# A decode block's feed-forward weights: w2 thirteen rows to a partition, w1 in two transfers, h1 in two passes

## The chip, the core and the metric

The kernel runs on one core of a Trainium2 chip. The metric is the device time of one execution in microseconds, the median of several runs. A core has TensorE (PE; the loads of its stationary operand are shown as PEld), VectorE (DVE), ScalarE (ACT), GpSimd (POOL) and SyncE (SP), and 16 DMA engines that move data between HBM and SBUF.

## The reference

One decode step of a transformer block for 4 sequences: attention over a cache of 4096 positions with 32 heads of 128, then a feed-forward layer with the Mish activation, both with a layer norm ahead and a residual.

```python
x = A_x                                             # 4 x 1 x 640, bf16
h = x + _A_ref(_layernorm(x), k_cache, v_cache, wq, wo)
h2 = h + _B_ref(_layernorm(h), w1, b1, w2)          # w1 640 x 1728, w2 1728 x 640

def _B_ref(x, w1, b1, w2):
    h = x @ w1 + b1
    sp = log1p(exp(-abs(h))) + where(h > 0, h, 0)
    return (h * tanh(sp)) @ w2
```

The caches hold 2 x 4 x 32 x 4096 x 128 bf16 values, 268 MB of the 283 MB that the kernel reads.

## The kernel before

The attention runs over 16 units (`u`, eight heads of one sequence). For each, K (8.4 MB, `kt`) and V (`vt`) are loaded into one of three large SBUF slots by SP's queue (`load_kv`, L89). VectorE multiplies K by q (L263), TensorE adds up over the head dimension (L270), VectorE reduces (L251), softmax follows, and TensorE multiplies by V (`pv`, L325). The order is written out by hand (`manual_schedule`), and each engine runs its instructions in the order of the program.

The end of the kernel is where the change lies. When the last K has been used, its slot becomes `wend`, which takes the four blocks of wo (L388) and then w1 (L389); when the V before the last has been used, its slot becomes `wend2`, which takes w2 (L396, L397, L399) and all the small buffers of the end (`scratch`). The last V comes in four quarters. All of these are issued by SP in this order, and the DMA engines serve SP's queue in order.

w1 has 640 rows, which stand as five blocks of 128 partitions (`dc`), each row 1728 columns. The 1728 columns of h1 are cut into chunks of 128, thirteen of them and a fourteenth of 64 (`FREM`). `f_chunk(rows, c)` gives the columns of chunk c; before, these are adjacent columns. The result h1 has the columns of a chunk on its partitions, the chunk and the sequence in the free dimension: `h1_ps[f, c, n]`. For each chunk the five blocks are added up (L491), with w1 as the stationary operand, a load of 128 x 128 for each matmul of 4 columns. After the fifth chunk comes the variance of the layer norm (L469, with Sqrt at L501 and a switch of ACT's table to Exp at L504). VectorE and ScalarE then scale, add b1 and apply Mish (L511 to L537), and y2T (L547) multiplies by w2, whose row for partition p of chunk c must be the same f. b1 is brought into the same order by 14 small matmuls near the start (L213), also by `f_chunk`. The residual (L555), a transpose (L559) and a copy (L567) lead to the output DMA (L568).

w2 is loaded before as one row to a partition and chunk: chunk 12 (`w2s_sb`), then the 64 odd rows (`w2r_sb`), then three groups of four chunks.

Of the kernel before, what the change touches and what calls it, by code (L numbers as in the profile page):

```python
# [16 lines left out]
def kernel(  # L17
# [13 lines left out]
    nc = tc.nc  # L31

    B, Sq, D = A_x.shape
    _, H, Sk, Dh = A_k_cache.shape
    F = B_w1.shape[1]
    N = B * Sq
    DC = D // 128
# [16 lines left out]
    CT = 128 // (G * RQ)  # L54
    VQ = 4

    CI = 4
    CK = F // (128 * CI)
    FM = CK * CI * 128
    C2 = F // 128  # L60
    FREM = F - C2 * 128
    FC = C2 + 1

    ctx.enter_context(tc.manual_schedule())

# [13 lines left out]
    def slot(name):  # L79
        return slots.tile([128, SLOT], BF16, tag="kv", name=name)  # L80
# [36 lines left out]
    nc.vector.memset(nscale[:, :], -SCALE)  # L117
    b1T = consts.tile([128, FC], FP32)
    nc.gpsimd.memset(b1T[:, :], 0.0)
# [38 lines left out]
    for src, dst in ((ln1_v, xT), (x_v, xT_res)):  # L158
# [10 lines left out]
        out=own1[:, :], in_=ident[:, :].rearrange("p (i k) -> p i k", i=G), axis=AX.X, op=ALU.add  # L169
    )  # L170
    nc.vector.tensor_scalar(
        out=own[:, :], in0=own1[:, :], scalar1=-1.0, scalar2=1e30, op0=ALU.add, op1=ALU.mult
    )
    nc.vector.tensor_reduce(
        out=sel[:, :, :],
        in_=ident[:, :].rearrange("p (t i r) -> p r i t", t=CT, r=RQ),
# [5 lines left out]
        out=dq_f[:, :], in_=ident[:, :].rearrange("p (q j) -> p q j", j=J), axis=AX.X, op=ALU.add  # L182
# [4 lines left out]
        out=j_f[:, :], in_=ident[:, :].rearrange("p (q j) -> p j q", j=J), axis=AX.X, op=ALU.add  # L187
# [1 line left out]
    nc.vector.tensor_copy(out=j_m[:, :], in_=j_f[:, :])  # L189

    def f_chunk(rows, c):
        if c < CK * CI:
            k, i = divmod(c, CI)
            block = rows[:, k * 128 * CI : (k + 1) * 128 * CI]
            return block.rearrange("p (i f) -> p i f", i=CI)[:, i, :], 128
        return rows[:, c * 128 : min(F, (c + 1) * 128)], min(F - c * 128, 128)


    qT_ps = ps.tile([128, H, N], FP32, tag="qq", name="qT_ps")
    for h in range(H):  # L200
        for c in range(DC):
# [4 lines left out]
                start=(c == 0),  # L206
                stop=(c == DC - 1),
            )
    nc.scalar.copy(out=qT[:, :, :], in_=qT_ps[:, :, :])
    b_ps = ps.tile([128, FC], FP32, tag="oT", name="b_ps")  # L210
    for c in range(FC):
        cols, fw = f_chunk(b1_row, c)
        nc.tensor.matmul(  # L213
            b_ps[0:fw, c : c + 1], lhsT=cols, rhs=ident[0:1, 0:1], start=True, stop=True
        )
    nc.vector.tensor_copy(out=b1T[:, 0:C2], in_=b_ps[:, 0:C2])  # L216
    nc.vector.tensor_copy(out=b1T[0:FREM, C2:FC], in_=b_ps[0:FREM, C2:FC])

# [165 lines left out]
    w1_sb = wend[:, nwo : nwo + DC * F].rearrange("p (c f) -> p c f", c=DC)  # L384
    e0 = nwo + DC * F
    wo_view = A_wo.rearrange("(o p j) n -> p o j n", o=NO, j=J)
    for o in range(NO):
        nc.sync.dma_start(out=wo_sb[:, o], in_=wo_view[:, o])  # L388
    nc.sync.dma_start(out=w1_sb, in_=B_w1.rearrange("(c p) n -> p c n", p=128))  # L389
    wend2 = slot("wend2")  # L390
    nw2 = FC * D
    w2_sb = wend2[:, 0 : CK * CI * D].rearrange("p (k i n) -> p k i n", k=CK, i=CI)
    w2s_sb = wend2[:, CK * CI * D : C2 * D]
    w2r_sb = wend2[0:FREM, C2 * D : FC * D]
    w2_view = B_w2[0:FM, :].rearrange("(k i p) n -> p k i n", k=CK, i=CI)
    nc.sync.dma_start(out=w2s_sb, in_=B_w2[FM : C2 * 128, :])  # L396
    nc.sync.dma_start(out=w2r_sb, in_=B_w2[C2 * 128 : F, :])  # L397
    for k in range(CK):
        nc.sync.dma_start(out=w2_sb[:, k], in_=w2_view[:, k])  # L399

    at = [nw2]

    def scratch(n, dt=FP32):
        a = at[0]
        w = n * (2 if dt == FP32 else 1)
        w += w % 2
        at[0] = a + w
        ap = wend2[:, a : a + w]
        return ap.bitcast(FP32)[:, 0:n] if dt == FP32 else ap[:, 0:n]
# [53 lines left out]
    def column_means(src, name):  # L463
        part = scratch(N)
        nc.vector.tensor_reduce(
            out=part, in_=src.rearrange("p c n -> p n c"), axis=AX.X, op=ALU.add
        )
        m_ps = ps.tile([128, N], FP32, tag="oT", name=f"{name}_ps")
        nc.tensor.matmul(m_ps[:, :], lhsT=mean_f, rhs=part, start=True, stop=True)  # L469
        return m_ps  # L470
# [4 lines left out]
    for dst in (h2T, hc):  # L475
        nc.vector.tensor_tensor(
            out=dst,
# [7 lines left out]
    h1_ps = ps.tile([128, FC, N], FP32, tag="qq", name="h1_ps")  # L485
    nc.vector.memset(h1_ps[FREM:128, FC - 1, :], 0.0)
    rstd = scratch(N)
    for c in range(FC):
        fw = f_chunk(w1_sb[:, 0, :], c)[1]
        for dc in range(DC):  # L490
            nc.tensor.matmul(  # L491
                h1_ps[0:fw, c, :],
                lhsT=f_chunk(w1_sb[:, dc, :], c)[0],
                rhs=h2T[:, dc, :],
                start=(dc == 0),
                stop=(dc == DC - 1),
            )
        if c == 4:
            v_ps = column_means(sq, "var")
            std = scratch(N)  # L500
            nc.scalar.activation(  # L501
                out=std, in_=v_ps[:, :], func=ACT.Sqrt, bias=eps_t[:, :], scale=1.0
            )
            nc.scalar.activation(out=dummy[:, :], in_=eps_t[0:N, :], func=ACT.Exp)  # L504
            nc.vector.reciprocal(out=rstd, in_=std)

    def fcn():
        return scratch(FC * N).rearrange("p (c n) -> p c n", c=FC)
# [3 lines left out]
        out=h1n,  # L512
# [6 lines left out]
        out=h1s,  # L519
# [8 lines left out]
        out=tb, in0=ta, scalar=2.0, in1=ta, op0=ALU.add, op1=ALU.mult  # L528
# [3 lines left out]
        out=tc_, in0=tb, scalar1=-0.5, scalar2=-1.0, op0=ALU.mult, op1=ALU.add  # L532
# [5 lines left out]
        out=act_t, in0=td, scalar=1.0, in1=h1s, op0=ALU.add, op1=ALU.mult  # L538
    )

    y2T = ps.tile([128, DC, N], FP32, tag="s", bufs=4, name="y2T")
    w2_of = [(w2s_sb, CK * CI), (w2r_sb, C2)]
    w2_of += [(w2_sb[:, c // CI, c % CI, :], c) for c in range(CK * CI)]
    for i, (w2, c) in enumerate(w2_of):
        rows = 128 if c < C2 else FREM
        for dc in range(DC):
# [4 lines left out]
                start=(i == 0 and dc == 0),  # L551
                stop=(i == FC - 1 and dc == DC - 1),
# [3 lines left out]
        out=oT.rearrange("p n c -> p c n"), in0=hT, in1=y2T[:, :, :], op=ALU.add  # L556
# [6 lines left out]
        start=True,  # L563
        stop=True,
# [35 lines left out]
```

## Time and profile before

| | |
|---|---|
| median of 3 runs | 669.94 us (669.81 to 670.23) |
| the profiled execution | 670.03 us, of which the span from first to last instruction is 668.3 us |
| busy in the span | PE 383.0, PEld 179.8, DVE 353.2, ACT 86.8 us |
| moved by DMA | 283.78 MB, on average 425 GB/s |
| last 5% of the span | wo, w1 and w2 land; h1, Mish and y2T |

The DMA engines are busy for nearly all of the span, and the chain of work that ended last consists for the most part of K's loads and VectorE's multiplication. In the lines of the profile a time in front is the start in us from the span's beginning; `x25` is a number of instructions; what stands in brackets is how long the engine had been idle and which instruction ended that; `out<-in` are the program's names; L491 is line 491 of the kernel. In a view by stretches the columns are busy time and number of instructions of PE, PEld, DVE, ACT and POOL, then TensorE's granted clock, the busy share of the DMA engines, and GB/s.

### The profile page before, as it was taken

To read this page: it belongs to the slowest core of one execution; us is meant where nothing else is said; L and a number is where in the kernel's file an instruction comes from. 1 tells how busy PE (TensorE), PEld (TensorE's weight loads), DVE (VectorE), ACT (ScalarE), POOL (GpSimd) and SP (SyncE) were. 2 spreads that over 40 slices of the span, in tenths; PEclk is the share of its full clock that TensorE was granted. 3 is DMA by queue.
4 is the path that set the end of the run, shared out by engine and by line. 5 is a ranking of instruction groups with operands and counts; after the bars stand their busy time and mean duration, and the time that the engine had idled before them with its cause. 6 is when DMAs were issued, how large, how long until landed. Compare 5 with 4: busy or idle time off the path is not lost.

```text
span 668.3 us, 6430 instructions
## 1 busy us (share of the span) xinstructions
PE 383.0 (57%) x2793; PEld 179.8 (27%) x2793; DVE 353.2 (53%) x314; ACT 86.8 (13%) x314; POOL 1.4 (0%) x10
## 2 busy tenths in 40 slices
PE   0366758375572738557283765738285573728754
PEld 0222323132231313223031322313132231313343
DVE  2078848183663818366381935738192664818321
ACT  0102020202011020202002020110202011020211
POOL 0000000000000000000000000000000000000000
PEclk9998979679696968969698886979888696977965
DMA  9999999999999999999999999999999999999996
GB/s 377 440 439 432 439 433 432 436 428 429 428 436 435 429 432 432 432 436 432 432 432 437 436 421 435 432 436 432 432 428 432 435 432 439 432 440 399 423 415 208
DMA packets 8293, 283.78 MB, mean 425 GB/s; under 512 B 771, under 2 KB 2503, under 8 KB 3144
## 3 DMA queue, kind: packets, MB, share of 16 engines
q1 hardware_dynamic: 8254, 283.35, 98.7%
q8 instruction: 22, 0.36, 0.2%
q14 instruction: 7, 0.06, 0.0%
q10 hardware_dynamic: 10, 0.01, 0.0%
HBM read 283.35 MB, written 0.01 MB: 424 GB/s over the span
## 4 chain that ended last, share of the span: by engine, by line
DMA 59%; DVE 25%; PE 12%; issue 2%; SPq 0%; DVEq 0%; ACT 0%
DMA kt<-in_A_k_cache_dram 55%; DVE kt L263 21%; PE s L270 6%; DMA wend<-in_B_w_dram 5%; PE o L325 4%; DVE s_sb L251 3%; DVE pm L289 1%; PE tr L291 0%; PE tr L302 0%; DVE mx L295 0%; PE h_ps L491 0%; PE y2T L547 0%; SPq L388 0%; DVE otn L354 0%; DVE rl L353 0%
## 5 line engine op out<-in xcount | busy, mean ns | idle before, releaser
L270 PE MATMUL s<-kt,ident 128*128 128x512 bf16 x1024 | 269.7, 418 | 223.6 <-DVE kt L263 223.6
L263 DVE TENSOR_TENSOR kt<-kt,qb 128x4096 bf16<-128x4096 bf16 x128 | 288.1, 2283 | 191.1 <-DMA kt<-in_A_k_cache_dram 191.1
L270 PEld LDWEIGHTS <-ident 128*128 128x128 bf16 x1024 | 108.6, 106 | 378.3 <-issue 148.4
L309 ACT ACTIVATE e<-s_sb,nb 128x256 bf16<-128x256 f32 x128 | 63.1, 494 | 219.0 <-DVE nb L304 219.0
L251 DVE TENSOR_REDUCE s_sb<-s 128x64 f32<-128x512 f32 x64 | 43.9, 687 | 54.6 <-PE s L270 32.6
L325 PE MATMUL o<-vt,e 128*32 128x512 bf16 x1024 | 66.2, 416 | 4.4 <-DMA vt<-in_A_v_cache_dram 4.4
L237 ACT CAST qb<-qb_ps 128x128 bf16<-128x128 f32 x16 | 4.2, 265 | 306.4 <-PE qb_ps L229 306.4
L325 PEld LDWEIGHTS <-e 128*32 128x32 bf16 x1024 | 28.1, 104 | 34.4 <-issue 13.7
L309 ACT ACTIVATION_READ_ACCUMULATOR e<-s_sb,nb 128x1 f32 x128 | 23.8, 186 | 0.0
L291 PE MATMUL tr<-ident_f,pm 128*1 128x128 f32 x32 | 6.1, 270 | 21.3 <-DVE pm L289 21.3
L344 PE MATMUL oT<-sel,o_sb 128*128 128x8 f32 x128 | 17.5, 263 | 1.1 <-ACT o_sb L333 1.1
L344 PEld LDWEIGHTS oT<-sel,o_sb 128*128 128x128 f32 x128 | 16.4, 201 | 1.3 <-ACT o_sb L333 1.3
L353 DVE RECIPROCAL rl<-oT 128x8 f32<-128x8 f32 x16 | 3.2, 199 | 17.0 <-PE oT L344 17.0
L333 ACT COPY o_sb<-o 128x512 f32<-128x512 f32 x16 | 9.1, 569 | 14.7 <-PE o L325 14.7
L202 PE MATMUL qT_ps<-xT,first 128*128 128x4 bf16 x160 | 4.4, 167 | 10.0 <-DMA first<-in_A_wq_dram 10.0
L302 PE MATMUL tr<-mx,nscale 1*128 1x8 f32 x32 | 6.1, 262 | 5.9 <-DVE mx L295 5.9
L291 PEld LDWEIGHTS tr<-ident_f,pm 128*1 128x1 f32 x32 | 1.8, 80 | 28.7 <-issue 28.7
L295 DVE TENSOR_REDUCE mx<-tr 1x8 f32<-1x128 f32 x16 | 4.5, 279 | 9.0 <-PE tr L291 9.0
L302 PEld LDWEIGHTS tr<-mx,nscale 1*128 1x128 f32 x32 | 4.7, 183 | 10.6 <-DVE mx L295 10.6
L216 DVE COPY b1T<-b_ps 128x13 f32<-128x13 f32 x1 | 0.2, 173 | 13.4 <-PE b_ps L213 13.4
L202 PEld LDWEIGHTS <-first 128*128 128x128 bf16 x160 | 4.3, 104 | 10.1 <-DMA first<-in_A_wq_dram 10.1
L340 PEld LDWEIGHTS oT<-rs,ones_f 128*128 128x128 f32 x32 | 6.1, 198 | 3.3 <-issue 1.3
(77 smaller groups left out, 71.8 us busy)
## 6 DMA issues: line engine op xcount, KB each, us to landing
vt<-in_A_v_cache_dram SPq DMA_DIRECT2D x4, 2048.0 KB, 44.0
first<-in_A_wq_dram SPq DMA_DIRECT2D x1, 5120.0 KB, 15.5
wend<-in_A_wo_dram SPq DMA_DIRECT2D x4, 1280.0 KB, 21.3
wend<-in_B_w_dram SPq DMA_DIRECT2D x1, 2160.0 KB
wend<-in_B_w_dram SPq DMA_DIRECT2D x3, 640.0 KB, 17.8
kt<-in_A_k_cache_dram SPq DMA_DIRECT2D x16, 47.9
vt<-in_A_v_cache_dram SPq DMA_DIRECT2D x15, 35.2
wend<-in_B_w_dram SPq DMA_DIRECT2D x1, 160.0 KB, 28.2
```

Of the source, the lines that this page charges most:

```text
L202: nc.tensor.matmul(qT_ps[:, h, :], lhsT=wq_sb[:, c, h * Dh : (h + 1) * Dh], rhs=xT[:, c, :], start=(c == 0), stop=(c == DC - 1),)
L251: nc.vector.tensor_reduce(out=s_sbs[u][:, part * RP : (part + 1) * RP], in_=s_ps[:, :, :], axis=AX.X, op=ALU.add,)
L263: nc.vector.tensor_tensor(out=kt[:, :, d0 : d0 + DQ], in0=kt[:, :, d0 : d0 + DQ], in1=qbs[u][:, d0 : d0 + DQ].unsqueeze(1).to_broadcast([1 ...
L270: nc.tensor.matmul(s_ps[:, :, :], lhsT=ident[:, :], rhs=kt[:, :, d : d + W], start=(d == 0), stop=(d == Dh - W),)
L289: nc.vector.tensor_reduce(out=pm[:, :], in_=s_sb[:, :], axis=AX.X, op=ALU.max)
L291: nc.tensor.matmul(tr_ps[0:1, 0:128], lhsT=pm[:, :], rhs=ident_f[:, :], start=True, stop=True)
L302: nc.tensor.matmul(nb_ps, lhsT=nscale[:, :], rhs=mx[:, :], start=True, stop=True)
L309: nc.scalar.activation(out=e2[:, :, i, :], in_=s_sb[:, :].rearrange("p (g r) -> p g r", r=RQ), func=ACT.Exp, bias=nb[:, i : i + 1], scale= ...
L325: nc.tensor.matmul(o_ps[t : t + G * RQ, :], lhsT=e2[:, g, :, :], rhs=vt[:, g * RQ : (g + 1) * RQ, :], start=(g < CT), stop=(g >= NGV - CT),)
L333: nc.scalar.copy(out=o_sb[:, :], in_=o_ps[:, :])
L340: nc.tensor.matmul(oT_ps[:, 1, :], lhsT=ones_f[:, :], rhs=rss.pop(u)[:, :], start=True, stop=True)
L344: nc.tensor.matmul(oT_ps[:, 0, :], lhsT=o_sb[:, r * Dh : (r + 1) * Dh], rhs=sel[:, r, :], start=(r == 0), stop=(r == RQ - 1),)
```

## The change

Three things change together. Chunk c of the 1728 columns becomes every thirteenth column, starting from column c: partition p of chunk c is column 13p + c, and the 64 odd columns stay the last ones. So partition p needs the thirteen adjacent rows 13p to 13p + 12 of w2, and w2 is loaded in runs of 8, 4 and 1 rows to a partition, its 64 odd rows first; y2T goes through them in that order. The columns of w1 aren't moved in SBUF: the stationary operand of h1 is read from every thirteenth column, and so is the row of b1. w1 is loaded by two transfers, four blocks and the fifth, and h1 is made in two passes, first the four blocks for all chunks (with the variance after the fifth chunk as before), then the fifth block for all chunks, with the 64 odd columns first. The accumulation in PSUM is opened once by the first matmul and closed by the last.

```diff
-    CI = 4
-    CK = F // (128 * CI)
-    FM = CK * CI * 128
     C2 = F // 128
-    FREM = F - C2 * 128
+    FM = C2 * 128
+    FREM = F - FM
     FC = C2 + 1
+    W2P = (0, 8, 12, C2)
+    W1P = 4
...
     def f_chunk(rows, c):
-        if c < CK * CI:
-            k, i = divmod(c, CI)
-            block = rows[:, k * 128 * CI : (k + 1) * 128 * CI]
-            return block.rearrange("p (i f) -> p i f", i=CI)[:, i, :], 128
-        return rows[:, c * 128 : min(F, (c + 1) * 128)], min(F - c * 128, 128)
+        if c < C2:
+            return rows[:, 0:FM].rearrange("p (f k) -> p k f", k=C2)[:, c, :], 128
+        return rows[:, FM:F], FREM
...
-    nc.sync.dma_start(out=w1_sb, in_=B_w1.rearrange("(c p) n -> p c n", p=128))
+    w1_view = B_w1.rearrange("(c p) n -> p c n", p=128)
+    for c0, c1 in ((0, W1P), (W1P, DC)):
+        nc.sync.dma_start(out=w1_sb[:, c0:c1], in_=w1_view[:, c0:c1])
     wend2 = slot("wend2")
     nw2 = FC * D
-    w2_sb = wend2[:, 0 : CK * CI * D].rearrange("p (k i n) -> p k i n", k=CK, i=CI)
-    w2s_sb = wend2[:, CK * CI * D : C2 * D]
+    w2_sb = wend2[:, 0 : C2 * D].rearrange("p (k n) -> p k n", k=C2)
     w2r_sb = wend2[0:FREM, C2 * D : FC * D]
-    w2_view = B_w2[0:FM, :].rearrange("(k i p) n -> p k i n", k=CK, i=CI)
-    nc.sync.dma_start(out=w2s_sb, in_=B_w2[FM : C2 * 128, :])
-    nc.sync.dma_start(out=w2r_sb, in_=B_w2[C2 * 128 : F, :])
-    for k in range(CK):
-        nc.sync.dma_start(out=w2_sb[:, k], in_=w2_view[:, k])
+    w2_view = B_w2[0:FM, :].rearrange("(p k) n -> p k n", k=C2)
+    nc.sync.dma_start(out=w2r_sb, in_=B_w2[FM:F, :])
+    for k0, k1 in zip(W2P, W2P[1:]):
+        nc.sync.dma_start(out=w2_sb[:, k0:k1], in_=w2_view[:, k0:k1])
...
-    for c in range(FC):
+    def h1_pass(c, dcs):
         fw = f_chunk(w1_sb[:, 0, :], c)[1]
-        for dc in range(DC):
+        for dc in dcs:
             nc.tensor.matmul(
                 h1_ps[0:fw, c, :],
                 lhsT=f_chunk(w1_sb[:, dc, :], c)[0],
                 rhs=h2T[:, dc, :],
-                start=(dc == 0),
-                stop=(dc == DC - 1),
-            )
+                start=(c == 0 and dc == 0),
+                stop=(c == C2 - 1 and dc == DC - 1),
+            )
+
+    for c in range(FC):
+        h1_pass(c, range(W1P))
         if c == 4:
             v_ps = column_means(sq, "var")
...
+    for c in (C2, *range(C2)):
+        h1_pass(c, range(W1P, DC))
...
-    w2_of = [(w2s_sb, CK * CI), (w2r_sb, C2)]
-    w2_of += [(w2_sb[:, c // CI, c % CI, :], c) for c in range(CK * CI)]
+    w2_of = [(w2r_sb, C2)] + [(w2_sb[:, c, :], c) for c in range(C2)]
```

## The prediction, made before the changed kernel was run

> **What bounds the kernel now.** I read the chain of waits first, in order of time. Until 624 us it alternates between the loads of K and the score work on them, and none of that is touched. Its last pieces are what the change works on:
>
> ```profile
> 626.25 31.86 DMA wend<-in_B_w_dram
> ...
> 658.15 0.83 PE h_ps L491 x25
> 658.98 0.43 PE var_ps L469 x2
> 659.41 1.44 PE h_ps L491 x45
> 660.87 0.23 DVE wend L511
> ...
> 662.94 2.20 PE y2T L547 x70
> 665.16 0.23 DVE wend L555
> ```
>
> The first line is the transfer of w1, issued at 626.25 and landed at 658.11. TensorE starts h1 0.04 us later, so the landing of w1 sets everything behind it: 2.72 us of h1 (658.15 to 660.87), 2.07 us of activation (to 662.94), 2.22 us of y2T (to 665.16), then the output. Next, the DMA share and rate by stretch:
>
> ```profile
> 652.00:654.00 2.00, 1.23 (x40) 1.15 (x40) 0.32 (x2) 0.00 (x0) 0.00 (x0) 0.50 1.03 377
> 654.00:656.00 2.00, 0.56 (x2) 0.50 (x2) 0.70 (x6) 0.00 (x0) 0.00 (x0) 0.50 1.05 367
> 656.00:657.00 1.00, 0.00 (x0) 0.00 (x0) 0.00 (x0) 0.00 (x0) 0.00 (x0) 0.50 1.09 309
> 657.00:658.00 1.00, 0.00 (x0) 0.00 (x0) 0.00 (x0) 0.00 (x0) 0.00 (x0) 0.50 1.04 354
> ```
>
> The last column is GB/s, the one before it the busy share: the DMA engines are full while h1 waits, so w1 can't come sooner as a whole, only in parts. The completion records in the trace (each of 16 DMA engines counts a transfer done) say more: w1 is counted from 652.51 (first engine) to 658.11 (last); the wo block before it ended on that last engine at 652.33, so its w1 took 5.78 us. The five transfers of w2 are last counted at 658.66, 659.13, 660.65, 662.42 and 664.18. The last w2 piece is first used after 55 matmuls of y2T, at about 664.45: only 0.3 us of slack. Two chains thus run close together, w1 to h1 to activation to y2T, and the end of w2.
>
> The third view is the timeline of the loads of stationary operands, because the change alters how they read:
>
> ```profile
> 5.34 0.35 PE L161 MATMUL tp_ps<-ident,first 4*128 4x4 bf16 x5 [5.34 <-DVE first L141]
> 5.96 0.27 PE L161 MATMUL tp_ps<-ident,first 4*128 4x4 bf16 x5 [0.27 <-DVE xT L164]
> 6.36 0.27 DVE L168 TENSOR_REDUCE own<-ident 128x8 f32<-128x128 bf16 x1
> 7.42 0.37 DVE L186 TENSOR_REDUCE j_f<-ident 128x8 f32<-128x128 bf16 x1
> 658.15 0.74 PEld L491 LDWEIGHTS <-wend 128*128 128x128 bf16 x25 [3.49 <-DMA wend<-in_B_w_dram]
> ```
>
> The first L161 group loads columns 5 elements (10 bytes) apart, the second adjacent ones; both have 128 columns. In the single records the weight loads of the first follow each other at 40 ns, those of the second at 25 to 29. Likewise L186 reads the same 128x128 as L168, 16 bytes apart, and takes 370 ns for 274. In h1, with adjacent columns, load and matmul come every 26.7 ns (24 steps from 658.155 to 658.814, with the first wider); its five 64-column ones come every 53 ns.
>
> **The change part by part.**
>
> *w1 in two transfers.* Rows of 3456 bytes stay; four fifths land, by the 5.78 us, 1.16 us before the whole: 656.95, h1 starts at 656.99. What it needs else is there at 655.5 (L476, L465). The added transfer is a boundary in a full queue: the four quarters of vt15 are counted on the last engine at 625.20, 630.11, 635.00 and 639.92, 4.9 us for 2.1 MB or 427 GB/s, no gap to see. On SP the second w1 issue waits for the first quarter of vt15 (630.1); behind it stand the w2 issues, which before had to wait till 630.48 too, and the w2 data is wanted by the engines after 652.5. Hidden by 20 us.
>
> *h1 in two passes.* The same 70 matmuls: 65 of 128 columns and 5 of 64. One more change between the widths is added, 0.07 to 0.09 us by the gaps at 660.31 and 663.05. The fifth block lands at 658.1; the first pass, 56 matmuls with the variance in it, can't end before 656.99 + 52 x 0.0267 + 0.45 + 0.28 = 659.1, so its wait costs nothing (cover 1.0 us). The variance follows 20 matmuls, not 25, and the ACT table load behind it (1.28 us) starts earlier, so Exp isn't held. At unchanged pace h1 would end at 656.995 + 2.77 = 659.77, that is 1.10 before 660.87.
>
> *Columns 13 apart.* Chunk c is now every 13th column of w1, a step of 26 bytes, in all 65 wide loads; the odd 64 columns stay adjacent. No row has this step. The lower bound is 40 ns (L161 at 10 bytes: a wider step is no cheaper), the upper 107 ns: a load that falls to the pace of the 64-column ones, twice 53. Below nothing is excluded, as no strided row is faster than its adjacent one. Between the ends, the reduce rows say that the cost of a step is there at 16 bytes, +0.75 ns on some 1.08 ns an element (the slope of L251 against L168: 413 ns over 384 elements), a factor of 1.7: 46 ns. A straight line through 26.7 ns at 2 bytes and 40 at 10 says 67 at 26. The step lies between; I take the middle, 57 ns, +30.3 each: 65 x 30.3 = 1.97 us, all on the path, for TensorE does nothing else there. The 14 loads for b1 (L213) are strided too, at most 14 x 80 ns = 1.1 us later at 21 us; behind them is the issue of vt0 at 21.30, whose queue has kt0 and kt1 (16.8 MB) still to move, and qb0, which is needed at 36. Nothing.
>
> The Trainium skill, page "SBUF — State Buffer", section "Specifications (TRN2)", asks for two or more hits on each 16-byte line for full pace, which speaks against this change: at 26 bytes each column stands alone on its line, at L161's 10 bytes two of eight do. If L161's 13.3 ns belong to these, four times as many cost 53: 80 ns, an estimate, and the sum would be 672.2 us where my 57 gives 670.7.
>
> *w2 in long runs.* 1728 packets of 1280 bytes become 64 of 1280, 128 of 10240, 128 of 5120, 128 of 1280. Packet medians: 60 ns at 1280, 388 at 10240 (wo); 5120 by a line through 3456 (139) and 10240, 200. On the last engine w2r's 0.47 us (659.13 less 658.66), 8 x 388, 8 x 200, and 0.55 for a row as w2's single row took: 5.7 us behind w1 for 6.07 before: last landing 663.8 for 664.18. With y2T at 662.94 or later, all is there when it is used: worth 0 on the path. It bounds a gain: 5 matmuls and the drain after 663.8 put L555 at 664.1, so no more than 1.1 us can be won. If the packets were no faster than before (664.18), 0.7.
>
> *y2T.* The order now has one change of row count, not two; the pauses at 663.05 and 663.28 were 0.09 each: -0.09. The loads stay adjacent.
>
> Sum: -1.10 + 1.97 - 0.09 = +0.78 us. The profiled execution took 670.03 (span 668.3 and 1.7 around it), 0.09 above the median: 670.8 by its own time, 670.7 by the median.
>
> In terms of the pace s: time = 669.94 - 1.19 + 65 x (s - 0.0267). It is even at 45 ns, and 0.2% slower (1.34 us, about what a measurement of this kernel can tell from no change) at 66.
>
> **The rivals.**
>
> *Steep loads, slower.* Each wide load costs over 66 ns; at 87, the middle between the straight line and the 107, +60 each is 3.9 us: 672.7, at 107 674.0. For it: step 10 already costs half again, and 26 is 2.6 times as far. Against: L174 reads 64 bytes apart and takes 356 ns, no more than L186 at 16, so on VectorE the price stops growing. The skill's estimate of 80 belongs here.
>
> *The price stops at once.* 40 ns, as at 10 bytes: -1.19 + 0.86 = -0.33, 669.6. For it: L174 against L186. Against: it says that 10 bytes are as bad as it gets.
>
> *Free loads, faster.* 26.7 ns: bounded by w2's end, -1.1: 668.8. The page "TensorE: Matmul & The Clock Gate" of the Trainium skill, section "Weight-path perf modes — Fast Weight Load (FWL) and DoubleRow", has the fast load take its chunks "packed or strided", with steps up to 1,024 elements. L161's 40 ns, well under 107, agree that the fast load stays, and disagree that it stays at full pace.
>
> *The split does not bring the four blocks earlier.* The DMA engines' 5.6 us of spread between first and last could swallow it, were the last engine to serve both pieces together. Then 1.16 is lost: 671.9. Against: the quarters of vt15 are counted one by one.
>
> **How the numbers follow.** Middle pace, 46 to 66 ns, 0.40: 670.7, own range 670.0 to 671.3. Stops at 40, 0.21. Steep, 0.24. Free, 0.07. Split without effect, 0.08. Faster than 668.6 needs free loads and a w2 that lands sooner still: 0.06. Slower than 671.28: steep, most of the ineffective split, the top of the middle: 0.36. The rest, 0.58, within. Range 668.7 to 672.9: it holds the free and the 40 ns cases, the middle, and the steep one to 90 ns.
>
> **What would show it.** Right: h1's first matmul near 657.0, steps near 57 ns, the DVE wait for h1 ending near 661.7, the last w2 count near 663.8, y2T about 2.1 us without a pause for w2. Wrong: steps of 27, 40 or over 66 ns; h1 starting at 658; a pause in y2T that waits for w2's DMA.

## The result, and the profile after

The changed kernel takes 671.0 us (median of 22 runs) for 669.96 of the kernel before: 1.04 us more, a ratio of 1.0016 (95% interval 1.0009 to 1.0022). The forecast was 670.7 in a range of 668.7 to 672.9, with 0.58 for less than 0.2% either way. The profiled execution took 670.93 us (span 669.1) against 670.03.

The end of the chain of waits (start in us, duration in us, what), changed kernel:

```profile
626.13 30.73 DMA wend<-in_B_w_dram
...
656.90 1.34 PE h_ps L489 x20
658.25 0.43 PE var_ps L467 x2
658.67 3.16 PE h_ps L489 x50
...
661.86 0.23 DVE wend L514
...
663.93 2.11 PE y2T L549 x70
...
666.06 0.23 DVE wend L557
```

Three differences stand in it. h1 starts at 656.90 for 658.15, after the first four blocks of w1: 1.25 us won. From h1's start to the use of its result it takes 4.96 us (656.90 to 661.86) for 2.72: 2.24 lost. y2T takes 2.13 (663.93 to 666.06) for 2.22: 0.09 won. The sum is +0.90, all of the difference between the two profiled executions; the activation between h1 and y2T takes 2.07 us in both.

The same stretches as before, by engine (the last two columns are the DMA share and GB/s):

```profile
652.00:654.00 2.00, 1.25 (x41) 1.20 (x41) 0.36 (x2) 0.00 (x0) 0.00 (x0) 0.50 1.08 394
654.00:656.00 2.00, 0.54 (x2) 0.45 (x2) 0.65 (x5) 0.00 (x0) 0.00 (x0) 0.50 1.05 384
656.00:657.00 1.00, 0.10 (x2) 0.10 (x3) 0.00 (x0) 0.00 (x0) 0.00 (x0) 0.50 0.93 358
657.00:658.00 1.00, 1.00 (x19) 1.00 (x19) 0.00 (x0) 0.00 (x0) 0.00 (x0) 0.50 1.10 368
...
663.00:664.00 1.00, 0.07 (x3) 0.07 (x3) 0.81 (x3) 0.00 (x0) 0.00 (x0) 0.50 0.00 0
```

In 657 to 658, where the kernel before had TensorE idle, it now loads and multiplies, but only 19 matmuls fit into that microsecond. The DMA engines move 17, 17 and 49 GB/s more in the first three stretches than before, and from 663 on they are idle. The completion records agree: w1's first piece is last counted at 656.86, its second at 658.12, w2's four transfers at 658.64, 661.55, 663.05 and 663.48, the last for 664.18 before.

The weight loads of h1 (PEld) by duration, min/median/max in ns, of the kernel before and of the changed one:

```profile
L491 PEld LDWEIGHTS <-wend x70: 103/104/291, 658.2 to 660.6; 128*128 128x128 bf16 x65, 128*64 128x64 bf16 x5
```

```profile
L489 PEld LDWEIGHTS <-wend x70: 129/159/304, 656.9 to 661.6; 128*128 128x128 bf16 x65, 128*64 128x64 bf16 x5
```

A load that took 104 ns takes 159. The loads overlap, so what counts is the distance from one to the next. In the single records of the trace that is 58 to 64 ns, mostly 59 to 61, between wide matmuls, for 26.7 before.

### The profile page after: what moved, and what is told of

It is laid out like the page before. It is cut to its first block, busy times and chain, and to the rows that moved or that the text cites. A ratio compares the mean times of both kernels' runs of the same rounds, so it can differ in the third digit from the quotient of the medians.

```text
span 669.1 us, 6430 instructions
## 1 busy us (share of the span) xinstructions
PE 385.3 (58%) x2793; PEld 182.5 (27%) x2793; DVE 353.3 (53%) x314; ACT 86.8 (13%) x314; POOL 1.4 (0%) x10
## 4 chain that ended last, share of the span: by engine, by line
DMA 59%; DVE 25%; PE 12%; issue 2%; SPq 0%; DVEq 0%; ACT 0%
DMA kt<-in_A_k_cache_dram 55%; DVE kt L261 21%; PE s L268 6%; DMA wend<-in_B_w_dram 5%; PE o L323 4%; DVE s_sb L249 3%; PE h_ps L489 1%; DVE pm L287 1%; PE tr L289 0%; PE tr L300 0%; DVE mx L293 0%; PE y2T L549 0%; SPq L386 0%; DVE otn L352 0%; DVE rl L351 0%
```

## The experiments

**The step alone.** Does the loss come from the column step, or from the second transfer and the second pass? The first kernel keeps the step and the w2 of the changed one, with h1 in one pass as before:

```diff
-    w1_view = B_w1.rearrange("(c p) n -> p c n", p=128)
-    for c0, c1 in ((0, W1P), (W1P, DC)):
-        nc.sync.dma_start(out=w1_sb[:, c0:c1], in_=w1_view[:, c0:c1])
+    nc.sync.dma_start(out=w1_sb, in_=B_w1.rearrange("(c p) n -> p c n", p=128))
...
```

> The changed kernel with w1 in one transfer and h1 in one pass; the column step of 13 and w2's long runs stay. My theory: h1 starts at 658.1 as before, its 65 wide loads come every 60 ns for 26.7, so 2.2 us more, less 0.1 in y2T: 672.0. Rival (the two passes cost, the step little): 670.3 or less.

Measured: 672.09 us, ratio 1.0032 (1.0020 to 1.0045). Its timeline:

```profile
658.17 1.67 PE L487 MATMUL h_ps<-wend,wend 128*128 128x4 bf16 x25 [3.70 <-DMA wend<-in_B_w_dram]
660.13 2.88 PE L487 MATMUL h_ps<-wend,wend 128*128 128x4 bf16 x45
663.05 0.22 DVE L507 TENSOR_TENSOR wend<-h_ps,wend 128x56 f32<-128x56 f32 x1 [2.26 <-PE h_ps L487]
```

The 25 matmuls that took 0.83 us take 1.67, h1 as a whole 4.88 us for 2.72. The step costs 2.2 us, and the split of w1 gives about half of it back (671.0 for 672.09).

**The split alone.** The reverse: the kernel before, with w1 in two transfers and h1 in two passes.

> The kernel before with only w1 in two transfers and h1 in two passes; adjacent columns, w2 as before. My theory (the early landing of four blocks is worth 1.2 us, and only the column step costs): h1 starts near 656.9, steps of 26.7 ns, h1's result is taken near 659.8, y2T starts near 661.9; then w2 binds, whose last piece still lands near 664.2, so y2T's result is taken near 664.5 for 665.16: 0.65 us less than before, 669.3. Rival (the second pass and the second transfer are what costs in the changed kernel): 670.0 or more.

Measured: 669.77 us, ratio 0.9997 (0.9988 to 1.0006), where 669.3 was expected. The profile says why:

```profile
656.91 0.69 PE L494 MATMUL h_ps<-wend,wend 128*128 128x4 bf16 x20 [2.25 <-DMA wend<-in_B_w_dram]
657.89 1.79 PE L494 MATMUL h_ps<-wend,wend 128*128 128x4 bf16 x50
659.72 0.22 DVE L519 TENSOR_TENSOR wend<-h_ps,wend 128x56 f32<-128x56 f32 x1 [1.18 <-PE h_ps L494]
661.79 1.65 PE L555 MATMUL y2T<-wend 128*128 128x4 bf16 x50 [2.11 <-DVE wend L545]
664.15 0.70 PE L555 MATMUL y2T<-wend 128*128 128x4 bf16 x20 [0.71 <-DMA wend<-in_B_w_dram]
664.89 0.22 DVE L563 TENSOR_TENSOR wend<-wend,y2T 128x20 bf16<-128x20 f32 x1 [3.15 <-PE y2T L555]
```

h1 starts at 656.91 and ends at 659.72, 1.15 us ahead of before: the theory's part. y2T starts 1.15 us early as well, and then waits 0.71 us for w2's last transfer, which lands at 664.11 (664.18 before). I had put the end of y2T 0.3 us behind that landing; but the last transfer holds four chunks, so twenty matmuls come after it, and the result is taken 0.78 us behind it. The two chains lie as close together as the prediction said; of 1.15 us, 0.27 is left.

**The price of the step.** The kernel before, with each chunk of h1 read at a step of its own from 1 to 13:

```diff
-                lhsT=f_chunk(w1_sb[:, dc, :], c)[0],
+                lhsT=w1_sb[:, dc, 0 : 127 * (c + 1) + 1 : c + 1]
+                if c < C2
+                else f_chunk(w1_sb[:, dc, :], c)[0],
```

> The kernel before, with chunk c of h1 (c from 0 to 12) read from the columns 0, c+1, 2(c+1) and so on, so that the five loads of each chunk have a step of 1 to 13 elements; h1 is thus made of other columns than the reference's. My theory (1.9 ns for each 16 bytes opened by a quarter of the columns, at least 26.7 ns): 27, 27, 27, 30, 40, 46, 53, 60 ns for steps 1 to 8 and 60 for 9 to 13. Rival, a straight line: 27, 30, 33, 37, 40, 43, 47, 50 and on to 67 ns at 13. Rival, only columns alone on their 16 bytes are dear: 27 up to step 4, 40 at 5, and 60 from 8 on. The sum over the chunks makes the run about 1.3 us longer than before by the first, 1.4 by the second.

Measured, median distance between the matmuls of one chunk, from the single records:

```
step (elements)   1   2   3   4   5   6   7   8   9  10  11  12  13
step (bytes)      2   4   6   8  10  12  14  16  18  20  22  24  26
ns               27  27  27  33  39  47  54  62  59  59  57  60  60
```

Steps up to 6 bytes are free, from there to 16 bytes each further element costs 6 to 8 ns, and beyond 16 bytes nothing is added; 16 bytes is even the dearest step. Theory and table agree within 3 ns at each step; the straight line misses at 3 (33 for 27), at 8 (50 for 62) and at 13 (67 for 60). The second rival, columns alone on their 16 bytes, is off by 6 ns at step 4 (27 for 33), where the theory is off by 3; beyond that it named only 40 at 5 and 60 from 8 on, as the theory does. The theory's 60 ns from step 9 on were the changed kernel's, so what it foretold is the way up to there. The table thus gives the price, but not why it is so. In this kernel each step stands at its own place in the order; the kernels that use one step for many chunks show the same distances (27 at 1 and 3, 32 to 33 at 4, 61 to 62 at 8, 60 at 13). The one run took 671.05 us, 1.1 more than before (1.3 was expected; h1 with its wait took 4.01 us for 2.72, but began 0.28 us earlier):

```profile
657.87 0.93 PE L491 MATMUL h_ps<-wend,wend 128*128 128x4 bf16 x25 [3.35 <-DMA wend<-in_B_w_dram]
659.08 2.77 PE L491 MATMUL h_ps<-wend,wend 128*128 128x4 bf16 x45
```

The first 25 matmuls (steps 1 to 5) take hardly more than the 0.83 us of before, the other 45 take 2.77 us for 1.57.

The Trainium skill, page "SBUF — State Buffer", section "Specifications (TRN2)", asks for two hits on a 16-byte line for full pace. The bend of the table at 16 bytes agrees with lines of that size. Two hits are not quite enough, though: at 8 bytes a load takes 33 ns for 27. And a column alone on its line costs 57 to 62 ns, less than the 80 that the prediction had estimated from this rule.

**Runs of four rows.** If the step is what costs, a w2 in shorter runs lets w1 be read at a small step; w2's transfers go over the same groups:

```diff
-    W2P = (0, 8, 12, C2)
+    W2P = (0, 4, 8, 12, C2)
...
-        if c < C2:
-            return rows[:, 0:FM].rearrange("p (f k) -> p k f", k=C2)[:, c, :], 128
+        for k0, k1 in zip(W2P, W2P[1:]):
+            if k0 <= c < k1:
+                block = rows[:, k0 * 128 : k1 * 128]
+                return block.rearrange("p (f k) -> p k f", k=k1 - k0)[:, c - k0, :], 128
...
```

> The changed kernel with w2 in runs of 4, 4, 4 and 1 rows to a partition, so that a chunk of w1 is every fourth column (8 bytes) and the last one adjacent. My theory (a load is paid by how much of the memory its columns are spread over, about 1.9 ns for each 16 bytes that a quarter of them opens, and not below 26.7 ns in all): 27 to 31 ns a load, h1 done near 660.0, w2's last piece near 663.9, y2T's result taken near 664.3: 669.1 to 669.3. Rival (a straight line in the step, 1.67 ns a byte): 37 ns, h1 done near 660.5, 669.6. The Trainium skill, page SBUF - State Buffer, section Specifications (TRN2), asks for two hits on a 16-byte line, which four columns 8 bytes apart just give: 26.7 ns by that.

Measured: 669.23 us, ratio 0.9989 (0.9981 to 0.9998): faster than before by 0.7 us, with the loads of h1 32 to 33 ns apart, between the expected 27 to 31 and the straight line's 37.

```profile
657.04 0.81 PE L491 MATMUL h_ps<-wend,wend 128*128 128x4 bf16 x20 [2.36 <-DMA wend<-in_B_w_dram]
660.20 0.22 DVE L516 TENSOR_TENSOR wend<-h_ps,wend 128x56 f32<-128x56 f32 x1 [1.40 <-PE h_ps L491]
662.27 2.09 PE L551 MATMUL y2T<-wend 64*128 64x4 bf16 x70 [2.11 <-DVE wend L542]
664.40 0.22 DVE L559 TENSOR_TENSOR wend<-wend,y2T 128x20 bf16<-128x20 f32 x1 [2.18 <-PE y2T L551]
```

y2T runs through without a pause, its result is taken 0.76 us earlier than before (664.40 for 665.16).

**Runs of three rows**, where the step is free: `W2P = (0, 3, 6, 9, 12, C2)`.

> The changed kernel with w2 in runs of 3, 3, 3, 3 and 1 rows to a partition, w1 read at a step of 3, which in the step curve costs nothing. Against the version with runs of 4: 60 loads of 33 ns become 27, 0.36 us; w2 lands near 663.7, its last five matmuls are wanted from 663.6 on, so up to 0.1 us of that is lost: 668.9. Rival (w2's end already binds the version with runs of 4): 669.2.

Measured: 669.04 us, ratio 0.9988 (0.9980 to 0.9997), the shortest median of all, between the expected 668.9 and the rival's 669.2. Against the kernel before, measured beside each, runs of three are 0.84 us shorter and runs of four 0.73: too close for the medians to tell apart. h1 takes 2.87 us (657.11 to 659.98), 0.29 less than with runs of four, and its loads come about 27 ns apart.

```profile
657.11 0.71 PE L491 MATMUL h_ps<-wend,wend 128*128 128x4 bf16 x20 [2.37 <-DMA wend<-in_B_w_dram]
659.98 0.22 DVE L516 TENSOR_TENSOR wend<-h_ps,wend 128x56 f32<-128x56 f32 x1 [1.22 <-PE h_ps L491]
662.05 2.09 PE L551 MATMUL y2T<-wend 64*128 64x4 bf16 x70 [2.11 <-DVE wend L542]
664.18 0.22 DVE L559 TENSOR_TENSOR wend<-wend,y2T 128x20 bf16<-128x20 f32 x1 [2.18 <-PE y2T L551]
```

**Eight, four and one, each for itself.** The w2 transfers of the changed kernel, with steps 8, 4 and 1 in place of 13: `W2P = (0, 8, 12, C2)` in the grouped version.

> The changed kernel with the same three w2 transfers (8, 4 and 1 rows to a partition), but each laid out for itself: w1 is read at a step of 8 in chunks 0 to 7, 4 in 8 to 11, 1 in the twelfth. By the step curve just measured (62, 33 and 27 ns): 40 x 2 more, 20 x 27 and 5 x 33 less than in the changed kernel's 60 ns, 0.6 us less in all: 670.4. Rival (the price rises with the step in bytes even beyond 16 bytes, so that 13 is dearer than 8 and these 40 loads get cheaper by a quarter): 670.0 or less.

Measured: 670.35 us, ratio 1.0008 (0.9999 to 1.0017). h1 from 656.91 to 661.22 is 4.31 us, 0.65 less than in the changed kernel. The expectation (670.4) holds, so the 16-byte step is as dear as the 26-byte one.

**Is the length of w2's runs worth anything?** The changed kernel with w2's rows 32 bytes apart in SBUF, so that nothing but the run length changes:

```diff
...
-    w2_sb = wend2[:, 0 : C2 * D].rearrange("p (k n) -> p k n", k=C2)
+    DP = D + 16
+    w2_sb = wend2[:, 0 : C2 * DP].rearrange("p (k n) -> p k n", k=C2)[:, :, 0:D]
...
```

> The changed kernel with w2's rows 32 bytes apart in SBUF, so that the same transfers go in runs of 1280 bytes again. If long runs are off the path there (y2T starts at 663.9 only, after all of w2 has landed): w2's last piece lands near 664.2 for 663.5, before the last five matmuls want it at 665.8, and the time stays at 671.0. Rival (the shorter w2 also lets w1 land sooner, and so is on the path): 671.3 or more.

Measured: 670.84 us, ratio 1.0015 (1.0006 to 1.0024), the changed kernel's own result. The profile shows that the runs are short again: these are the lines on DMA packets of the changed kernel and of this one.

```profile
DMA packets 7013, 283.78 MB, mean 424 GB/s; under 512 B 771, under 2 KB 967, under 8 KB 1736
```

```profile
DMA packets 8293, 283.78 MB, mean 424 GB/s; under 512 B 771, under 2 KB 2503, under 8 KB 3144
```

w2's last piece lands at 664.09 for 663.48, and y2T, from 664.26 on, doesn't see it. The same padding in the version with runs of three, where w2's end is near:

> The version with runs of 3 rows, with the rows 32 bytes apart in SBUF, so that w2 goes in runs of 1280 bytes. If the long runs count as soon as h1 is early: w2's last piece lands near 664.2, y2T pauses for it and its result is taken near 664.5: 669.3, 0.4 more than the version with long runs. Rival (run length is nothing to the end, only the one-row last piece is): 668.9 too.

Measured: 669.04 us, ratio 0.9988 (0.9980 to 0.9997), no different from the version without padding; the expected 0.4 us did not come. In its profile w2 still lands 5.74 us behind w1 (657.79 to 663.53), for 5.42 with long runs (658.36 to 663.78); but there w1 had landed 0.57 us sooner, and y2T was held for only 0.13 us (2.22 us for 2.09). Whether w1 came sooner by chance (w1's last landing lies between 657.8 and 658.5 in these profiles) or because of the short runs behind it, single profiles can't say; the medians say that the run length is worth less than can be measured.

**The tail of w2.** The version with the split alone, with the one-row chunk `w2s_sb` last instead of first, in the transfers and in y2T.

> The version with only w1 split and h1 in two passes, with w2's one-row chunk moved from the first place to the last, in the transfers and in y2T; adjacent columns and one row to a partition as before. There y2T had to do twenty matmuls after the last landing at 664.1, now it is five: its result is taken near 664.45 for 664.89, so 669.3, 0.4 less than the split alone. Rival (the wait for w2 is of bytes alone, so the order gives nothing): 669.8.

Measured: 669.49 us, ratio 0.9995 (0.9986 to 1.0004). In the profile the order counts, but it brought 0.23 us (result taken at 664.66 for 664.89), not 0.4; by the medians, each against the kernel before measured beside it, it is 0.19 (0.38 us shorter for 0.19), which their 95% intervals don't tell apart. The transfer ahead of the last, of four chunks, landed at 663.74, and 25 matmuls are behind it.

```profile
661.83 1.43 PE L556 MATMUL y2T<-wend 64*128 64x4 bf16 x45 [2.11 <-DVE wend L545]
663.79 0.83 PE L556 MATMUL y2T<-wend 128*128 128x4 bf16 x25 [0.53 <-DMA wend<-in_B_w_dram]
```

**Three pieces of w1**, on the version with runs of three, with w2 in four transfers (odd rows, six chunks, six chunks, one), to see whether h1 or w2 ends last there.

> The version with runs of 3 rows, with w1 in three transfers (3, 1 and 1 blocks) and h1 in three passes; w2 in four transfers. If the end of w2 binds there: h1 starts near 655.9 and is taken near 659.0, y2T starts near 661.0 and pauses for w2, whose last piece lands near 663.6 as before; result taken near 664.0: 668.9, no more than 0.15 less than with two pieces. Rival (h1 is still the later chain): y2T's result comes 0.9 us earlier, 668.1.

Measured: 669.23 us, ratio 0.9991 (0.9982 to 0.9999). h1 is taken at 658.78, 1.2 us sooner than with two pieces, and all of that is lost in a pause:

```profile
658.78 0.22 DVE L520 TENSOR_TENSOR wend<-h_ps,wend 128x56 f32<-128x56 f32 x1 [1.72 <-PE h_ps L494]
660.85 1.16 PE L555 MATMUL y2T<-wend 64*128 64x4 bf16 x35 [2.11 <-DVE wend L546]
663.04 1.09 PE L555 MATMUL y2T<-wend 128*128 128x4 bf16 x35 [1.03 <-DMA wend<-in_B_w_dram]
664.17 0.22 DVE L563 TENSOR_TENSOR wend<-wend,y2T 128x20 bf16<-128x20 f32 x1 [3.38 <-PE y2T L555]
```

The second six chunks land at 663.00 and have 35 matmuls behind them; the result comes at 664.17, as with two pieces (664.18). So w2's arrival is the floor here, and an earlier h1 gives nothing. This version also has w2 in larger pieces, with more matmuls behind each landing, and its median is 0.2 us above that of two pieces (669.04). But the trace of the version with two pieces says the same of that one: its fourth group of three chunks lands at 663.37 and is used from 663.47, its last chunk at 663.78 and is used from 663.87, so w2 leaves it about 0.1 us to win.

## Why the prediction was right

*w1 in two transfers*: right. h1 was to start at 656.99 and starts at 656.90; the whole DMA stream ran 0.2 us earlier in this execution (wo's last count at 652.12 for 652.33). The runs with and without the split (672.09 and 671.0) put it at 1.1 us on medians.

*Two passes*: right. The added change of width, put at 0.07 to 0.09 us, is there at 0.07 to 0.1 (steps of 0.125 and 0.128 us at the changes of width), and the second pass, from 660.75 on, never waits for the fifth block, landed at 658.12. The sum, though, carried only 0.05 for it (2.77 for 2.72); the split alone took 2.81.

*Columns 13 apart*: the sign and the place were right; the term was mis-sized. The pace is 60 ns where 57 was taken, so 65 x 3 ns or 0.2 us too little, which the earlier start of h1 half made up in the profile. The path to 57 was weaker than the number: it was the middle between a factor taken from VectorE (46) and a straight line (67), and the table of steps follows neither. That the middle came within 3 ns of the measured pace is luck. The cost rises more steeply than the straight line between 6 and 16 bytes, and stops there; its start, L161's 40 ns at 10 bytes, was read rightly (39 in the table). The lower bound's reason, that a wider step is no cheaper, does not quite hold: 16 bytes cost 62 ns, 22 bytes 57. What the prediction quoted against steep loads, that L174 at 64 bytes costs VectorE no more than L186 at 16, holds in the same way for TensorE's loads from 16 to 26 bytes.

*The loads for b1*, put at nothing: right. They come 61 ns apart for 27, the issue of vt0 moves from 21.30 to 21.82 us, and the first multiplication of K starts at 35.99 for 36.03.

*w2 in long runs, worth nothing on the path*: right, and shown by taking the long runs away (670.84). The last landing was put at 663.8, 5.7 us behind w1, and came at 663.48, 5.4 behind. *The bound on any gain*, 1.1 us from w2's end, is where the best versions stop: 0.84 us for runs of three, by medians, with a result at 664.18 in the profiled execution, the slowest of its eleven, where the bound had 664.1. The prediction counted 55 matmuls of the kernel before ahead of w2's last piece; there are 50, and the time that it gave, 664.45, is that of the 51st. That twenty follow it, and not fifteen, changes nothing in the prediction's sum, which has only five behind the last piece of the changed kernel; it is what the expectation of the split alone left out.

*y2T*, -0.09: as measured.

Of the rivals, free loads (27 ns), a price that stops at 40 and steep loads (over 66) are out by the 60 ns, and the split without effect by the start of h1.

## What to carry to other kernels

A rearrangement that makes a transfer's runs longer can be paid for by the engine that reads the other operand of the same index. Look at which side is on the path: here the long runs bought nothing that could be measured, and the strided weight loads cost 2.2 us. Where two chains end close together, an earlier start of one is worth only what lies between them, and how much work stands behind the last landing (twenty matmuls or five) decides how much that is.

## What the runs showed of the hardware

The distance between loads of 128 bf16 columns depends on the step between columns: 27 ns up to 6 bytes, 33 at 8, 39 at 10, 47 at 12, 54 at 14, and 57 to 62 from 16 to 26 bytes. The prediction had not foreseen that it is flat at the start and at the end. Every step stays well under 107 ns, twice the 53 ns between 64-column loads.

Where it can be compared (steps of 2, 10 and 26 bytes), the distance is the same at another granted clock and with fewer rows. The table was taken with 128 rows at a granted clock of 0.50. The loads for b1 have one row, at a granted clock of 1.00 (the stretch below is the changed kernel's), and there too come 27 ns apart with adjacent columns and 61 at a step of 26 bytes; L161's four rows come 40 ns apart at 10 bytes, also at 1.00.

```profile
20.60:21.60 1.00, 1.00 (x21) 0.97 (x18) 0.00 (x0) 0.56 (x2) 0.00 (x0) 1.00 0.15 66
```
